# Attention's first loads all on SP's queue in the order of the jobs; ScalarE keeps only tables, rms_g and three weight chunks ahead of its copies

## Chip, cores, metric

One core of one Trainium2 chip. The metric is the device time of one execution in microseconds (us), median over runs. Engines: PE is TensorE's matmul, PEld its weight load, DVE VectorE, ACT ScalarE, POOL GpSimd, SP SyncE. ACT and SP both issue DMAs; "ACTq" and "SPq" are these issues in the profile. A load has landed when its data is in place and its completion counter says so; an engine stands when it waits at an instruction of its program.

## The reference, cut to what matters

```python
# attention: batch 8, heads 8, seq 576, head_dim 64, all float32
scores = scale * np.matmul(q, k.transpose(0, 1, 3, 2))
ret = scores * Dmat[None]            # decay gamma**(i-j) where i >= j, else 0
attn = np.matmul(ret, v)
# bridge to (4608, 512), then a gated FFN with d_ff 1536
xn = x / rms * rms_g
out = (silu(xn @ w_gate) * (xn @ w_val)) @ w_out
```

The weights reach the kernel as 64-bit floats (1 MB per chunk of 128 x 4 x 256), and DVE and ACT decode them to float32 on the chip.

## The kernel before: the parts that matter

Attention is cut into 32 jobs (one batch, two heads). The first four jobs load q and k untransposed, and PE transposes them; ACT copies the transposes out of PSUM. One core does the whole of it, with all instructions of an engine in program order.

```python
def load_first(j):                       # q, k of jobs 0..3: six DMAs, always on SP
    ...
    for nm, src in (("q", q), ("k", k)):
        for e in range(2):
            nc.sync.dma_start(out=st[j][nm][:, :, e], in_=src[b, 2*hp+e, :NFULL*P]...)
        nc.sync.dma_start(out=st[j][nm + "t"], in_=...)

def load_kv(j, queue):                   # here only v and its tail: four DMAs
    ...

def turn(j):                             # PE transposes, ACT copies, ACT scales v
    last = bank(...)
    for i, nm in enumerate("qk"):
        ps = bank(...)
        for c in range(NFULL):
            nc.tensor.transpose(out=ps[:, c*P:c*P+P], in_=d[nm][:, c]..., identity=ident)
        nc.tensor.transpose(out=last[:, o], in_=d[nm + "t"]..., identity=ident[:TAIL, :TAIL])
        nc.scalar.copy(out=t[:, :NFULL*P], in_=ps)
        nc.scalar.copy(out=t[:, NFULL*P:], in_=last[:, o])
    scale_v(j)

def load_chunk(i):                       # one 1 MB chunk of a weight, on ACT
    ...
    nc.scalar.dma_start(out=dst, in_=src[rws, cols].rearrange("(c p) f -> p c f", p=P))

def start():
    ...
    load_first(0)
    load_kv(0, nc.scalar)
    for i in (2, 3, 0, 1, 4):            # gv, gt, causal, causal_t, gc
        table(i)                         # on ACT
    load_first(1)
    load_chunks(1)                       # chunk 0
    load_kv(1, nc.scalar)
    load_first(2)
    table(5)                             # gq, 512 KB
    load_chunks(2)                       # chunk 1
    load_kv(2, nc.scalar)
    load_first(3)
    nc.scalar.dma_start(out=rms_g, in_=...)
    load_chunks(3)                       # chunk 2
    turn(0)                              # ACT's first copy stands here
    for j in range(NHP):
        slot(j)                          # scores, states, weighing, values of job j
        if j + 1 < NHP:
            turn(j + 1)
        ...                              # exponent(0), exponent(1) after slot 0: decoding starts
```

A DMA from ACT or SP has to take one of eight completion counters, which the compiled program gives out in turn to both queues. An issue stands until the load that held its counter before has landed. The packed trace holds the counter (semaphore) of every issue: eight of them, numbers 100 and 102 to 108, serve both queues in all kernels here.

## Time and profile before

| | before |
|---|---|
| median of 4 runs beside the changed kernel | 1278.45 us (1277.49 to 1279.64) |
| span of the profiled run | 1275.3 us |
| ACT's first copy | 28.05 us |
| first scores on PE | 29.30 us |
| first product of the up stage on PE | 76.68 us |
| start of PE's unbroken stretch | 164.32 us |

The last four rows are start times in the timelines, counted from the span's start. The last two are these lines of PE's timeline (start, length, engine and line, operation, count; in brackets the idle time before and what ended it):

```profile
76.68 12.29 PE L470 MATMUL up<-x,w_gate 128*128 128x384 f32 x32 [0.71 <-DVE x L382]
...
164.32 10.56 PE L470 MATMUL up<-x,w_gate 128*128 128x384 f32 x32 [0.80 <-ACT w_gate L548]
```

From the second of them on PE does not stop for anything worth naming until the end. These two marks serve as milestones: a gain at the start is a gain in the time only if it is still there at the second.

### The profile page before, as it was taken

Reading aid. Unit: us, or ns where it says so; the run is one execution under the profiler, and the core shown is the slowest. Engines: PE = TensorE matmul, PEld = TensorE weight load, DVE = VectorE, ACT = ScalarE, POOL = GpSimd, SP = SyncE. Lnnn points to the kernel's source line nnn. Section 1 sums busy time; section 2 is a strip of 40 time slices with the busy share of each in tenths; the row PEclk is TensorE's granted clock in tenths of the full one; section 3 lists DMA queues with packets and bytes.
Section 4 is the critical chain, followed back from the end, with each engine's and each line's share of the span. In section 5 each row is a group of like instructions: output and inputs, shape, how many; then the busy total and the mean of one; then the engine's idle time right before and its main releaser. Section 6 shows DMA issues by size and latency. Waiting matters only on the chain.

```text
span 1275.3 us, 16411 instructions
## 1 busy us (share of the span) xinstructions
PE 1219.4 (96%) x6792; PEld 925.8 (73%) x6792; DVE 547.5 (43%) x1056; ACT 280.0 (22%) x520; POOL 43.0 (3%) x44
## 2 busy tenths in 40 slices
PE   1789799999999999999999999999999999999998
PEld 1556555546985994985994995895895896795893
DVE  0679873013552553343453453343443443343340
ACT  1746452011120211211211221121121121111110
POOL 0000003140000000000000000000000000000000
PEclk9889799999999999999999999999999999999999
DMA  9448730022121132002112223002032100000000
GB/s 220 110 107 203 170 111 22 9 61 53 38 52 47 37 73 53 9 1 61 37 37 53 46 40 79 17 1 53 14 69 52 40 7 10 17 1 17 9 1 25
DMA packets 225307, 65.68 MB, mean 51 GB/s; under 512 B 212688, under 2 KB 212816, under 8 KB 225232
## 3 DMA queue, kind: packets, MB, share of 16 engines
q1 hardware_dynamic: 212224, 44.23, 17.1%
q10 hardware_dynamic: 13008, 20.39, 5.0%
q8 instruction: 53, 0.87, 0.3%
q14 instruction: 22, 0.18, 0.0%
HBM read 55.16 MB, written 9.44 MB: 51 GB/s over the span
## 4 chain that ended last, share of the span: by engine, by line
PE 88%; DVE 4%; DMA 3%; ACT 3%; issue 1%; ACTq 0%; POOL 0%; SPq 0%; DVEq 0%; POOLq 0%
PE out L484 29%; PE x L413 12%; PE w L413 12%; PE z L413 12%; PE up L470 6%; PE y L413 6%; PE s L242 3%; PE av L292 2%; PE av L306 2%; DMA w_out<-in_moe_w_gate_dram 1%; PE s L252 1%; DMA v<-in_v_dram 1%; PE ms L360 1%; ACT w_gate L548 1%; PE rb L380 1%
## 5 line engine op out<-in xcount | busy, mean ns | idle before, releaser
L484 PE MATMUL out<-w_out,h 128*128 128x512 f32 x792 | 346.1, 594 | 0.0
L484 PEld LDWEIGHTS out<-w_out,h 128*128 128x128 f32 x792 | 149.1, 190 | 177.5 <-issue 175.1
L489 ACT COPY o_all<-out 128x512 f32<-128x512 f32 x36 | 21.1, 585 | 348.9 <-PE out L484 334.9
L420 DVE TENSOR_TENSOR u<-m,y 128x384 f32<-128x384 f32 x60 | 33.2, 554 | 149.8 <-PE y L413 141.8
L264 DVE TENSOR_TENSOR ret<-s,causal 128x1024 f32<-128x1024 f32 x32 | 39.1, 1223 | 133.0 <-PE av L292 69.0
L413 PE MATMUL x<-x,w_gate 128*128 128x192 f32 x480 | 88.9, 328 | 1.5 <-ACT m L437 1.5
L413 PE MATMUL x<-x,w_val 128*128 128x192 f32 x480 | 89.1, 329 | 0.0
L413 PE MATMUL z<-x,w_gate 128*128 128x192 f32 x480 | 87.8, 326 | 0.0
L413 PE MATMUL w<-sums,w_val 128*128 128x192 f32 x480 | 87.8, 326 | 0.0
L413 PE MATMUL w<-sums,w_gate 128*128 128x192 f32 x480 | 87.8, 326 | 0.0
L413 PE MATMUL z<-x,w_val 128*128 128x192 f32 x480 | 87.8, 326 | 0.0
L413 PEld LDWEIGHTS x<-x,w_gate 128*128 128x128 f32 x480 | 79.2, 190 | 7.1 <-issue 4.3
L413 PEld LDWEIGHTS x<-x,w_val 128*128 128x128 f32 x480 | 78.8, 190 | 1.4 <-ACT m L437 1.4
L413 PEld LDWEIGHTS z<-x,w_gate 128*128 128x128 f32 x480 | 79.7, 190 | 0.0
L413 PEld LDWEIGHTS w<-sums,w_gate 128*128 128x128 f32 x480 | 79.7, 190 | 0.0
L413 PEld LDWEIGHTS w<-sums,w_val 128*128 128x128 f32 x480 | 79.7, 190 | 0.0
L413 PEld LDWEIGHTS z<-x,w_val 128*128 128x128 f32 x480 | 79.7, 190 | 0.0
L280 ACT ACTIVATE sd<-sum,gc 64x256 f32<-64x256 f32 x64 | 32.3, 504 | 200.2 <-DVE sum L274 199.8
L470 PE MATMUL up<-x,w_gate 128*128 128x384 f32 x192 | 67.8, 514 | 1.5 <-ACT w_gate L548 0.8
L420 DVE TENSOR_TENSOR h<-u,w 128x384 f32<-128x384 f32 x60 | 33.3, 554 | 81.4 <-PE w L413 81.4
L432 ACT ACTIVATE h<-h 128x384 f32<-128x384 f32 x90 | 47.0, 523 | 88.6 <-DVE h L420 88.6
L382 DVE SCALAR_TENSOR_TENSOR x<-x,rms_g,rb 128x384 f32<-128x384 f32 x48 | 26.3, 608 | 89.2 <-PE rb L380 89.2
(98 smaller groups left out, 1349.2 us busy)
## 6 DMA issues: line engine op xcount, KB each, us to landing
out_dram<-o_all SPq DMA_DIRECT2D x36, 256.0 KB, 2.0
k<-in_k_dram SPq DMA_DIRECT2D x64, 128.0 KB, 2.9
qraw<-in_q_dram SPq DMA_DIRECT2D x112, 72.0 KB, 2.4
kraw<-in_k_dram SPq DMA_DIRECT2D x112, 72.0 KB, 2.6
v<-in_v_dram SPq DMA_DIRECT2D x58, 128.0 KB, 2.8
w_out<-in_moe_w_gate_dram ACTq DMA_DIRECT2D x6, 1024.0 KB, 6.2
w_out<-in_moe_w_val_dram ACTq DMA_DIRECT2D x3, 1024.0 KB, 5.6
w_gate<-in_moe_w_val_dram ACTq DMA_DIRECT2D x3, 1024.0 KB, 5.7
```

Source lines behind the costliest of these rows:

```text
L242: nc.tensor.matmul(s[:, e, ck] if c < NFULL else s[e * n : e * n + n, 2, :n], lhsT=d["kT"][r, ck], rhs=d["qT"][r, ck], start=True, stop=True,)
L264: nc.vector.tensor_tensor(out=ret.rearrange("p e (c k) -> p e c k", c=NFULL), in0=s[:, :2].rearrange("p e (c k) -> p e c k", c=NFULL), in1 ...
L280: nc.scalar.activation(out=sd[j % 2][r, :, r], in_=t[r], func=AF.Copy, scale=gc[r, hp : hp + 1])
L292: nc.tensor.matmul(av[blk][e * D : e * D + D, o : o + n], lhsT=d["v"][:, c, e] if c < NFULL else d["vt"][r], rhs=d["ret"][:, e, c * P : c ...
L306: nc.tensor.matmul(av[blk][:, o : o + n], lhsT=sd[j % 2][:, c - 1], rhs=d["qT"][:, c * P : c * P + n], start=False, stop=(c in (AC - 1, NC ...
L382: nc.vector.scalar_tensor_tensor(out=x[:, c], in0=x[:, c], scalar=rms_g[:, c : c + 1], in1=rb[:, :U], op0=ALU.mult, op1=ALU.mult,)
L413: nc.tensor.matmul(ps[:, i * HU : i * HU + HU], lhsT=w_up[m][:, 2 * blk + c, cut], rhs=t_of[u][blk][:, c], start=(start and i == c == 0), ...
L420: nc.vector.tensor_tensor(out=o, in0=a, in1=pairs_of(ps), op=ALU.add)
L432: nc.scalar.activation(out=o, in_=c, func=AF.Silu)
L470: nc.tensor.matmul(ps[:, :U], lhsT=w_up[m][:, 4 * half + c, i * P : i * P + P], rhs=x_of[u][:, c], start=(c == 0), stop=(c == NHP - 1),)
L484: nc.tensor.matmul(ps[:, :DM], lhsT=h_of[u][:, f, s * P : s * P + P], rhs=w_out[:, f], start=(f == 0), stop=(f == NF - 1),)
L489: nc.scalar.copy(out=o, in_=ps[:, :DM])
```

## The change

Intent: SP issues all of attention's loads, in the order in which the jobs use them, and ACT gets to its first copy earlier.

```diff
-        load_first(0)
-        load_kv(0, nc.scalar)
+        for j in range(NHP):
+            load_first(j)
+            if j + 1 < NHP:
+                load_kv(j)              # now always on SP
         for i in (2, 3, 0, 1, 4):
             table(i)
-        load_first(1)
-        load_chunks(1)
-        load_kv(1, nc.scalar)
-        load_first(2)
+        load_chunks(2)
         table(5)
-        load_chunks(2)
-        load_kv(2, nc.scalar)
-        load_first(3)
         nc.scalar.dma_start(out=rms_g, in_=moe_rms_g.rearrange("(c p) -> p c", p=P))
         load_chunks(3)
         turn(0)
```

`load_kv` loses its `queue` argument and uses `nc.sync`.

## The prediction

> **What bounds the kernel now.** I read the page first (PE 96% busy), then a table of busy time over four stretches, which shows where the other 4% are. Its columns are the stretch in us, its length, then busy us (x instructions) of PE, PEld, DVE, ACT and POOL, the granted clock, the DMA share and GB/s.
>
> ```profile
> 0.00:29.00 29.00, 2.69 (x10) 1.78 (x10) 0.34 (x6) 2.23 (x4) 1.63 (x8) 1.00 0.95 217
> 29.00:77.00 48.00, 33.18 (x296) 26.66 (x296) 29.55 (x60) 30.47 (x54) 0.86 (x1) 0.85 0.36 90
> 77.00:165.00 88.00, 78.49 (x426) 50.18 (x426) 76.08 (x117) 47.38 (x64) 0.85 (x1) 0.89 0.77 185
> 165.00:1275.30 1110.30, 1105.07 (x6063) 847.13 (x6061) 441.50 (x875) 199.89 (x400) 39.67 (x34) 1.00 0.16 35
> ```
>
> From 165 us to the end PE is busy 1105 of 1110 us: that part is PE's and the change touches none of its instructions. The first 165 us are a start-up in which PE is idle for 29.00-2.69 = 26.3, then 14.8, then 9.5 us. In the first 29 us no compute engine does anything to speak of while the DMA engines are 95% busy. So the question is what keeps the compute engines waiting there. The chain of waits over the first 60 us, in order (start, length, what), says it:
>
> ```profile
> 0.73 0.51 ACTq L175
> ...
> 1.27 4.13 DMA v<-in_v_dram
> ...
> 7.54 5.97 DMA w_out<-in_moe_w_gate_dram
> ...
> 13.53 3.61 DMA h<-in_q_dram
> ...
> 17.16 6.76 DMA w_out<-in_moe_w_gate_dram
> ...
> 23.94 2.84 DMA v<-in_v_dram
> ...
> 26.78 1.26 ACT L203
> ...
> 28.05 0.58 ACT qT L203
> ```
>
> The timelines of ACT (its DMA issues and its first work) and of PE in the same stretch:
>
> ```profile
> 26.21 0.52 ACTq L528 DMA_DIRECT2D w_out<-in_moe_w_val_dram  x1
> 26.76 1.28 ACT L203 ACT_TABLE_LOAD   x1 [26.76 <-DMA v<-in_v_dram]
> 28.05 0.58 ACT L203 COPY qT<-turn_q 128x512 f32<-128x512 f32 x1
> ...
> 6.62 1.12 PE L193 MATMUL turn_k<-ident,k 128*128 128x128 f32 x4
> 28.81 0.36 PE L198 MATMUL turn_t<-ident,h 64*128 64x64 f32 x1 [21.07 <-ACT qT L204]
> ```
>
> PE has job 0's q and k transposed by 7.7 us, and then stands for 21.07 us because ACT has not copied them out of PSUM. ACT has not, because the copy stands in its program behind 22 DMA issues (v of three jobs, six tables, rms_g, three weight chunks), the last at 26.21. Each of those issues waits for one of eight completion counters that both queues use in turn, as the compiled order with its waits shows; so an issue on ACT stands until an older load, often a 1 MB chunk, has landed. The copy itself needs nothing that comes after 7.7 us.
>
> **What the Trainium skill says.**
> "DMA: Bandwidth & Descriptors", section "Anatomy of one DMA": a semaphore wait of a DMA is waited out on the issuing sequencer, not in the DMA engine. The trace agrees: ACT issues the second half of job 2's v at 23.94, 0.02 us after chunk 1, issued at 17.16, has landed (17.16 + 6.76), and nothing of ACT runs in the gap before it.
> Same page, "Issuing engines are not separate DMA queues": all issuers share the same 16 DMA engines, so moving a load between SP and ACT saves only sequencer time. Here it says that no bandwidth is gained: the DMA share is 0.95 in the first 29 us. What can be gained is the sequencer's blocking, and that is far more than issue time here.
> "ScalarE: Activation LUTs", "What ACT_TABLE_LOAD costs": about 1283 ns. The trace has 1.28 us between the last issue and the first copy; the change keeps it.
> "TensorE: Matmul & The Clock Gate", "The HAM clock gate": half clock after idle windows of about 3.4 us that run freely. The trace agrees in kind: four transposes take 1.08 to 1.12 us up to 35 us and 0.61 at 44 us. A start that is shifted meets these windows elsewhere.
>
> **The change, part by part.**
> Removed from ACT ahead of its first copy: 12 issues, four for each of jobs 0 to 2 (v in two halves, vt in two halves). By themselves they are 1.10 + 1.20, 1.10 + 1.82 and 2.37 + 1.18 us in ACT's timeline, some waits included, so under 9 us; what counts is that of the 18 issues that wait for a counter before the first copy, 5 are left.
> Added to SP: the same 12 issues, interleaved per job (q, k, v; then the next job). Total bytes, number of DMAs and everything after the start-up are the same: the comparison of the two compiled orders shows PE, DVE and POOL in the same order, SP 12 issues longer before v of job 3, ACT 12 shorter.
> Moved: chunk 1 now directly follows chunk 0; gq, rms_g, chunk 2 follow, then the copy.
>
> When does ACT reach its copy afterwards? The compiled order of the changed kernel gives its waits. Five tables: no wait. Chunk 0 waits for q of job 0, first half; chunk 1 for q's tail; gq for v of job 0, first half; rms_g for job 0's vt; chunk 2 for q of job 1, first half, and that load, on SP, waits in turn for chunk 0. So one chain of three landings sets it, with durations from the table of DMA issues:
> - q of job 0 issued at 0.74, landing 3.1 us later: 3.8. (The five tables need 0.34+0.34+0.48+0.69+0.45 plus gaps, 2.5 us from 0.73: 3.2, so they don't bind.)
> - chunk 0 issued at 3.8; its landing took 6.0 us before beside loads of the other queue (5.2 to 6.8 for the three chunks): 9.8.
> - q of job 1 issued at 9.8; such loads took 3.1 to 3.8 us alone and 5.0 to 6.4 beside a chunk; chunk 1 and gq (1.5 MB) are still on the way: 5.0, so 14.8.
> - chunk 2 issued at 14.8 instead of 26.21.
> The side waits come earlier: v of job 0 is issued near 5 and lands by 11, gq follows. Table load and copy keep their distance of 1.84 us, so the first copy is at about 16.6 instead of 28.05: **11.4 us earlier**.
>
> Does all that follow shift as well? From 28 to 77 us the chain is copies, scores, weighing, states, then DVE's decoding of the weights, all behind each other in program order. The inputs have to be there at the shifted times. Job 1's k, second half, waits for chunk 1 (issued near 5, behind chunk 0 in its queue, landing near 13.5) and lands near 18.5; PE wants it at 34.11-11.4 = 22.7. Job 1's v is issued near 15 to 16, lands near 21; ACT scales it at 37.85-11.4 = 26.4. Job 2's k waits for chunk 2 (near 20) and lands near 25; PE wants it at 44.7-11.4 = 33.3. Chunk 2 itself is first read at 53.28-11.4 = 41.9. Margins of 4 to 20 us: the shift is carried whole. Later loads are triggered by compute (SP's v of job 3 by PE's values of job 0, chunk 3 by ACT's place in its program), so they shift too. After 165 us PE runs without gaps, so what is gained stays gained. Sum: 1279.1 - 11.4 = 1267.7, and I say 1267.5.
>
> **Rivals.**
> 1. *The counters take the waits' place.* SP's loads now wait for ACT's chunks and ACT's last chunk for SP's loads. If each of the three landings is at its slow end (3.7, 6.8, 6.4), chunk 2 is issued at 17.6 and the gain is 8.6 us: 1270.5. If at the fast end (2.9, 5.2, 3.6), at 12.4 and 13.8: 1265. For the slow end: two chunks now stand back to back in one queue beside six loads of job 0. For the fast end: in before, ACT's own 0.26 MB of v travelled beside q at the beginning.
> 2. *Attention's data arrive late.* All 36 loads are now on one queue in order; if the DMA engines, not ACT, set the start-up, job 1 or 2 would stand at its transposes and most of the gain goes back: perhaps 5 us left, 1274. For it: DMA share 0.95, some 220 GB/s over 6.7 MB in 30 us. Against it: the bytes needed before the copy fall (v of jobs 1 and 2, q and k of jobs 2 and 3 move behind it), and the margins above.
> 3. *The gain is lost in the weights' stage.* From 77 to 165 us DVE is 86% busy, the DMA engines 77%, and PE waits for weights. If that stage started at a fixed time, because chunks come at the rate of the DMA engines, the earlier start would be absorbed: 1277. Against it: chunks 3 on are issued by ACT behind its own work, and the DMA share from 29 to 77 us is only 0.36, so the data wait for the program.
> 4. *The clock.* Before, PE ran at half speed to about 40 us, and again near 137 to 153 us. Windows that fall otherwise give or take about 2 us.
>
> **Range and chances.** Rival 1 spans 1265 to 1270.5; the clock and the spread of the runs before (1277.5 to 1279.6) widen it by about 2.5 each way: 1262.5 to 1273. Faster by over 2% needs 25.6 us, and the first copy cannot come before about 8 us, 20 us earlier than now: 2%. Slower by over 2% would need a new wait of 25 us in the long stretch, whose order is unchanged: 1%. Within 2%: 97%.
>
> **What the changed profile would show.** Right: the ACT table load at 13 to 17 us; chunk 2's issue just ahead of it, ended by q of job 1; PE's wait for the copy shrunk from 21.07 to about 10 us; the jobs' first scores, PE's first up product (76.68) and the start of the unbroken PE stretch all about 11 us earlier. Wrong: PE waiting for k or v of job 1 or 2 (rival 2); the first up product earlier but the unbroken stretch beginning at the same 165 us (rival 3); chunk 2 issued after 19 us (rival 1 beyond my span).

## The result

| | before | after |
|---|---|---|
| median of 4 runs | 1278.45 us | 1266.28 us (1264.60 to 1266.58) |
| ratio | | 0.9902, 95% interval 0.9884 to 0.9919 |
| span of the profiled run | 1275.3 | 1264.4 |
| ACT's first copy | 28.05 | 16.56 |
| first scores | 29.30 | 17.80 |
| first up product | 76.68 | 65.47 |
| start of the unbroken stretch | 164.32 | 153.39 |

A ratio here is the mean time of one kernel's fast runs over that of the other's of the same rounds, so it is not quite the ratio of the medians quoted. It is 1% faster clear of noise.

ACT's timeline after, up to its first copy:

```profile
3.27 2.15 ACTq L528 DMA_DIRECT2D w_out<-in_moe_w_gate_dram  x2
13.57 0.35 ACTq L617 DMA_DIRECT2D gq<-gq_table  x1
14.24 0.43 ACTq L631 DMA_DIRECT2D rms_g<-in_moe_rms_g_dram  x1
14.73 0.51 ACTq L528 DMA_DIRECT2D w_out<-in_moe_w_val_dram  x1
15.26 1.28 ACT L203 ACT_TABLE_LOAD   x1 [15.26 <-DMA h<-in_q_dram]
16.56 0.59 ACT L203 COPY qT<-turn_q 128x512 f32<-128x512 f32 x1
```

Ten issues instead of 22; the last, chunk 2, now at 14.73 instead of 26.21, and the timeline names what ended ACT's wait: a load of q. That is q of job 1, which SP issued when chunk 0 had landed. The trace's semaphores show this chain on counter 102: q of job 0 (landed at 3.20), chunk 0 (issued at 3.27, landed at 9.77), q of job 1 (issued at 9.79, landed at 14.71), chunk 2 (issued at 14.73). SP's timeline has q of job 1 at 9.79, and PE's timeline of the same kernel follows:

```profile
9.79 0.93 SPq L157 DMA_DIRECT2D h<-in_q_dram  x2
...
22.17 0.93 SPq L157 DMA_DIRECT2D h<-in_q_dram  x2
```

```profile
10.11 1.09 PE L193 MATMUL turn_k<-ident,k 128*128 128x128 f32 x4 [4.24 <-DMA k<-in_k_dram]
17.31 0.37 PE L198 MATMUL turn_t<-ident,h 64*128 64x64 f32 x1 [6.11 <-ACT qT L204]
...
22.29 0.63 PE L193 MATMUL turn_k<-ident,k 128*128 128x128 f32 x4
...
65.47 12.39 PE L470 MATMUL up<-x,w_gate 128*128 128x384 f32 x32 [0.71 <-DVE x L382]
...
153.39 10.56 PE L470 MATMUL up<-x,w_gate 128*128 128x384 f32 x32 [0.80 <-ACT w_gate L548]
```

PE waits 6.11 us for ACT instead of 21.07, but 4.24 us for k of job 0, which did not matter before. All milestones have moved by about the same: the first copy by 11.49, the first scores by 11.50, the first up product by 11.21, the unbroken stretch by 10.93. The table by stretch says the same of the engines (columns as in the prediction's first table, the borders moved by about 11 us):

```profile
0.00:17.60 17.60, 2.76 (x10) 1.79 (x10) 0.34 (x6) 2.33 (x4) 1.64 (x8) 1.00 0.88 231
17.60:66.00 48.40, 31.28 (x296) 25.21 (x296) 29.75 (x61) 30.44 (x54) 0.87 (x1) 0.79 0.54 135
66.00:154.00 88.00, 78.24 (x426) 50.09 (x425) 75.92 (x116) 47.34 (x64) 0.85 (x1) 0.89 0.78 185
154.00:1264.40 1110.40, 1105.14 (x6063) 847.15 (x6062) 441.61 (x875) 200.18 (x400) 39.69 (x34) 1.00 0.16 35
```

Only the first stretch has become shorter. The second has the same work; its DMA share rises from 0.36 to 0.54 as part of the first loads, which used to be over by then, now runs beside it.

### The profile page after: what moved, and what is told of

Read it like the earlier page. It is cut to its first block, busy times and chain, and to the rows that moved or that the text cites. A ratio compares the mean times of both kernels' runs of the same rounds, so it can differ in the third digit from the quotient of the medians.

```text
span 1264.4 us, 16414 instructions
## 1 busy us (share of the span) xinstructions
PE 1217.4 (96%) x6792; PEld 924.2 (73%) x6792; DVE 547.6 (43%) x1056; ACT 280.3 (22%) x520; POOL 43.0 (3%) x44
## 4 chain that ended last, share of the span: by engine, by line
PE 88%; DVE 5%; ACT 3%; DMA 2%; issue 1%; SPq 1%; POOL 0%; DVEq 0%; ACTq 0%; POOLq 0%
PE out L484 29%; PE x L413 12%; PE w L413 12%; PE z L413 12%; PE y L413 6%; PE up L470 6%; PE s L242 3%; PE av L292 2%; PE av L306 2%; PE s L252 1%; DMA k<-in_k_dram 1%; ACT w_gate L548 1%; PE ms L360 1%; DVE w_gate L572 1%; DMA v<-in_v_dram 1%
```

## The experiments

The theory under test: the time hangs on the moment at which ACT is through its issues and starts copying; ACT is held there by loads of the other queue through the shared counters; the shift is then carried whole to the end. The rivals: the order of the loads brings the gain, or the data being there earlier; part of the shift is lost in the weights' stage; the clock decides. The ten new kernels and the second run of the changed one (e11) gave correct results. e11 is the changed kernel in the rounds of e9 and e10; it was expected at 1265 to 1267.5 us with a first copy at 15.5 to 17.5, and both came true.

| kernel | first copy | first scores | first up product | unbroken from | span | median us | ratio to before (95%) |
|---|---|---|---|---|---|---|---|
| before | 28.05 | 29.30 | 76.68 | 164.32 | 1275.3 | 1278.45 | |
| after | 16.56 | 17.80 | 65.47 | 153.39 | 1264.4 | 1266.28 | 0.9902 (0.9884, 0.9919) |
| e11, after again | 16.30 | 17.54 | 64.72 | 152.31 | 1263.3 | 1265.05 | 0.9886 (0.9871, 0.9901) |
| e1, queue alone | 15.89 | 17.14 | 65.35 | 153.55 | 1264.6 | 1265.78 | 0.9895 (0.9880, 0.9909) |
| e2, order alone | 26.37 | 27.62 | 74.33 | 161.98 | 1273.3 | 1275.91 | 0.9976 (0.9960, 0.9993) |
| e6, ACT held longer | 31.67 | 32.89 | 80.82 | 169.10 | 1280.1 | 1281.61 | 1.0017 (1.0002, 1.0032) |
| e4, one chunk ahead | 5.64 | 12.51 | 62.72 | 151.04 | 1262.0 | 1263.75 | 0.9871 (0.9856, 0.9886) |
| e5, no chunk ahead | 5.18 | 7.80 | 67.54 | 155.48 | 1266.5 | 1268.31 | 0.9906 (0.9891, 0.9921) |
| e8, after with PE kept warm | 16.94 | 18.18 | 63.39 | 151.60 | 1262.6 | 1264.08 | 0.9873 (0.9856, 0.9889) |
| e9, all on SP | 5.67 | 7.65 | 60.70 | 148.56 | 1259.7 | 1261.76 | 0.9859 (0.9845, 0.9874) |
| e10, e9 with PE kept warm | 5.17 | 8.01 | 62.11 | 150.86 | 1261.9 | 1262.75 | 0.9863 (0.9847, 0.9880) |
| e12, all on SP, woven | 5.16 | 7.80 | 57.35 | 144.73 | 1255.7 | 1257.49 | 0.9831 (0.9818, 0.9845) |
| e13, chunks on GpSimd | 5.12 | 20.29 | 67.44 | 155.05 | 1265.9 | 1267.60 | 0.9907 (0.9894, 0.9921) |

Two columns subtracted say most of it. Span minus start of the unbroken stretch lies between 1110.85 and 1111.3 in all thirteen profiles; start of the unbroken stretch minus first up product between 87.4 and 88.8. So whatever a kernel gains up to the first up product it keeps to within 1.4 us. Only what lies before it has to be explained.

### e1: the queue alone

```diff
-        load_kv(0, nc.scalar)      # and the same for jobs 1 and 2;
+        load_kv(0, nc.sync)        # all else in the order of before
```

> The order of before, with v of jobs 0 to 2 issued on SP instead of ACT, and nothing else. Theory (what counts is when ACT is through its issues, set by the chain q of job 0, chunk 0, q of job 1, chunk 2): its compiled waits hold the same chain, only gq and chunk 1 have changed places, so the first copy comes at 15.5 to 17.5 us (changed kernel 16.56, before 28.05) and the time is 1265 to 1268. Rival (the order of the jobs' loads and of the tables brings the gain): the order is that of before, so 1274 to 1279.

First copy 15.89, time 1265.78, ratio 0.9895: the time of the changed kernel. Once v is off ACT's queue, the order of the jobs' loads and tables in the program brings nothing more; taking v off is what makes the gain.

### e2: the order alone

```diff
             if j + 1 < NHP:
-                load_kv(j)                 # the changed kernel's order,
+                load_kv(j, nc.scalar)      # v issued on ACT
```

> The order of the changed kernel, but v of jobs 0 to 2 back on ACT, at the head of its program. Theory: ACT has its 22 issues again, but the chunks come last, so the 12 of v do not wait for chunks; at eight loads under way and some 3.5 us each I put the last issue at 17 to 21 us, the first copy at 19 to 23, the time at 1269 to 1273: between the two kernels. Rival (only the queue counts): 1277 to 1280. Rival (only the order counts): 1265 to 1267.

A miss in size: first copy at 26.37, not 19 to 23, and time 1275.91, not 1269 to 1273. ACT's timeline shows why:

```profile
13.45 1.89 ACTq L528 DMA_DIRECT2D w_out<-in_moe_w_gate_dram  x2
...
24.53 0.52 ACTq L528 DMA_DIRECT2D w_out<-in_moe_w_val_dram  x1
25.08 1.28 ACT L203 ACT_TABLE_LOAD   x1 [25.08 <-DMA k<-in_k_dram]
```

I had counted only how fast eight loads at a time get through. Twelve issues of v in front of the five tables start chunk 0 at 13.45 instead of 3.27, 10.2 us later. From there to chunk 2's issue it takes 24.53 - 13.45 = 11.1 us here, and 14.73 - 3.27 = 11.5 us in the changed kernel, but not through the same chain: by the trace's semaphores chunk 2 waits here for q of job 3, which SP issued at 15.99 without waiting for a chunk, and which took 8.5 us to land beside chunks 0 and 1. So v at the head of ACT's queue costs the 10.2 us; that the rest takes as long is not one mechanism. The order alone does gain a little, 0.24% (0.07 to 0.40).

### e6: the changed kernel with ACT held longer

```diff
         load_chunks(3)
+        pad = temp("pad").rearrange("p (a b) -> p a b", b=P)
+        for _ in range(27):
+            nc.scalar.activation(out=pad, in_=ones.unsqueeze(1).to_broadcast([P, NS, P]),
+                                 func=AF.Copy, scale=1.0)
         turn(0)
```

> The changed kernel with 27 idle copies on ACT (some 0.42 us each, 11.4 us together) between its last DMA issue and the first copy; all loads as in the changed kernel. Theory (all that follows hangs on the first copy, the shift is carried whole): first copy at 28, time 1277 to 1279, as before. Rival (the gain is in the loads, attention's data or chunks being there earlier): some of the delay is caught up, 1266 to 1273.

ACT's timeline:

```profile
16.83 14.93 ACT L635 ACTIVATE pad<-ones 128x384 f32<-128x384 f32 x27
31.67 0.57 ACT L203 COPY qT<-turn_q 128x512 f32<-128x512 f32 x1
```

The pad took 14.93 us rather than the 11.4 that I had worked out, 0.55 us for each copy and not 0.42; that is why the time lies above the expected 1277 to 1279. So the first copy came at 31.67, 15.11 us later than in the changed kernel, and the span grew by 1280.1 - 1264.4 = 15.7 us. Nothing is caught up, although the loads ahead of the first copy are as early as in the changed kernel (chunk 2 is issued at 14.98 against 14.73). "The data being there earlier" is ruled out as the source of the gain; the start of ACT's copies is.

### e4 and e5: fewer chunks ahead of the copies

```diff
-        load_chunks(2)                    # e4: load_chunks(1); e5: nothing
-        table(5)
-        rms_g, load_chunks(3)
         turn(0)
+        load_chunks(2); table(5); rms_g; load_chunks(3)
```

> The changed kernel, with chunk 1, gq, rms_g and chunk 2 issued behind job 0's copies; only the five tables and chunk 0 ahead. Theory (time follows the first copies): ACT is free at 5 us, so k of job 0 (landed at 8.4 to 11.3 us in the runs so far) becomes the bound; first scores at 10 to 12.5 us instead of 17.80, time 1258 to 1262. Rival (the chunks are needed early, and what they are issued later comes back as DVE waiting for them): 1264 to 1268 in spite of early scores.

> The changed kernel with all three chunks, gq and rms_g behind job 0's copies and scaling. Theory: k of job 0 lands without a chunk beside it, near 6.5; first scores at 8 to 9.5 us, 8.5 us earlier than in the changed kernel; chunk 0 is issued near 10, lands near 16, at most 1 to 2 us after DVE wants it; time 1256.5 to 1260.5. Rival (chunks needed early): DVE waits for chunk 0 and 1 by more than 3 us, ACT stands at its issues before job 1's copies, time 1260 to 1266, no better than with one chunk ahead.

Both have their scores about as early as expected, 12.51 and 7.80. Both missed their times: e4 lies between its two ranges, and e5 is above both of its own: with its scores 10 us earlier it is no faster than the changed kernel. The line of job 0's `sd` (its scaled state, which ACT computes between job 0's copies and job 1's) in ACT's timeline, of e4 and of e5, after the issue of chunk 2:

```profile
21.16 0.50 ACTq L528 DMA_DIRECT2D w_out<-in_moe_w_val_dram  x1
21.76 1.02 ACT L280 ACTIVATE sd<-sum,gc 64x256 f32<-64x256 f32 x2 [8.15 <-DMA h<-in_q_dram]
```

```profile
25.31 0.37 ACTq L528 DMA_DIRECT2D w_out<-in_moe_w_val_dram  x1
25.79 1.02 ACT L280 ACTIVATE sd<-sum,gc 64x256 f32<-64x256 f32 x2 [16.89 <-DMA h<-in_k_dram]
```

ACT's stand has not gone; it has moved from ahead of job 0's copies to between job 0's and job 1's, 8.15 us in e4 and 16.89 in e5. The wait is ACT's, at an issue, for a counter: in e5 chunk 2's issue at 25.31 follows the landing of a load of job 2's k at 25.29 on the same counter. The rival, DVE waiting for late chunks, is not what happened in e4, where DVE waited 0.2 us for one. In e5 it did come true, and so did ACT's stand, which the same rival had named: DVE waited 1.98 and 6.13 us for chunks 0 and 1. DVE's timeline of e5:

```profile
22.63 0.69 DVE L544 TENSOR_SCALAR w_gate<-w_out 128x1024 uint32<-128x1024 uint32 x1 [6.13 <-DMA w_out<-in_moe_w_gate_dram]
```

That wait was over at 22.63 and ACT's only at 25.79, so ACT's is the one that held up job 1.

### e9 and e12: no chunk on ACT at all, in two orders on SP

```diff
-        nc.scalar.dma_start(out=dst, in_=...)                        # in load_chunk
+        (nc.sync if i < 3 else nc.scalar).dma_start(out=dst, in_=...)
-            nc.scalar.dma_start(out=t, in_=src.ap())                 # in table
+            (nc.sync if i == 5 else nc.scalar).dma_start(out=t, in_=src.ap())
# e9:  tables, job 0, job 1, chunks 0 1, q k of job 2, gq, v of job 2, job 3, chunk 2, rms_g
# e12: tables, job 0, chunk 0, job 1, chunk 1, q k of job 2, gq, v of job 2, chunk 2, job 3, rms_g
```

> The changed kernel, with chunks 0 to 2, gq and rms_g on SP too, in the order job 0, job 1, chunks 0 and 1, job 2's q and k, gq, job 2's v, job 3, chunk 2, rms_g; ACT issues only the five small tables before its copies and nothing between job 0's and job 1's. Theory (the time follows the first scores as long as ACT does not stand at an issue): first scores near 7.8 us as with no chunk ahead, ACT free of the 8 to 17 us stand ahead of sd of job 0, chunks 0 and 1 landing near 18 and 21, at most 1 to 2 us late for DVE; time 1256 to 1260. Rival (the chunks are needed early and their place on the queue, not ACT's stand, made the runs with late chunks lose): DVE waits for them, 1262 to 1268.

> As the run with all loads on SP, with the chunks woven in where they are wanted: job 0, chunk 0, job 1, chunk 1, job 2's q and k, gq, job 2's v, chunk 2, job 3, rms_g. In the former run DVE waited 4.62, 2.10 and 3.09 us for chunks 0, 1 and 2 and the first product of the up stage came at 60.70 instead of 65.47. If the order is what was wrong there, these waits shrink to under 4 us together and the time is 1257 to 1260.5; if the loads as a whole are the bound by then (6.7 MB in the first 37 us), the waits only change place: 1260.5 to 1263.

In e9 ACT does not stand at an issue any more, scores start at 7.65, and yet the time fell only to 1261.76, between the theory's range and the rival's (from 1262). The mechanism is the rival's: DVE waits for chunks. DVE's timeline of e9:

```profile
18.29 0.69 DVE L544 TENSOR_SCALAR w_gate<-w_out 128x1024 uint32<-128x1024 uint32 x1 [4.62 <-DMA w_out<-in_moe_w_gate_dram]
21.09 0.69 DVE L544 TENSOR_SCALAR w_gate<-w_out 128x1024 uint32<-128x1024 uint32 x1 [2.10 <-DMA w_out<-in_moe_w_gate_dram]
...
37.04 0.69 DVE L544 TENSOR_SCALAR w_gate<-w_out 128x1024 uint32<-128x1024 uint32 x1 [3.09 <-DMA w_out<-in_moe_w_val_dram]
```

So once ACT is out of the way, the loads themselves are the next bound, and their order counts. e12 weaves the chunks in where they are wanted. DVE's waits for DMAs, from its list of waits up to 66 us in e12:

```profile
DVE w_gate L544 <- DMA w_out<-in_moe_w_gate_dram: 5.7, 1, 5.7
...
DVE x L315 <- DMA gq<-gq_table: 1.2, 1, 1.2
```

The total is 6.9 us against 6.7 + 3.1 + 1.8 = 11.6 in e9 by the same list; chunks 1 and 2 are no longer waited for. First up product at 57.35, time 1257.49, ratio 0.9831: the best of all, 1.7% faster than before and clearly faster than the changed kernel (0.9886 to 0.9902). I had expected these waits under 4 us together; chunk 0 is still 5.7 us late, without the time being out of its range.

### e13: chunks on GpSimd's queue

```diff
-        nc.scalar.dma_start(out=dst, in_=...)                        # in load_chunk; gq and rms_g too
+        (nc.gpsimd if i < 3 else nc.scalar).dma_start(out=dst, in_=...)
```

> The changed kernel with chunks 0 to 2, gq and rms_g issued by GpSimd, whose loads share no counter with the other two queues, so that neither ACT nor SP waits for a chunk. Theory: ACT does not stand; 3.5 MB of chunks and gq run beside job 0's loads from about 3 us on, so k and v of job 0 land late, at 10 to 13 us; first scores at 11 to 14 us, no wait of DVE for chunks, time 1259 to 1263. If the counters did not matter and the landing of job 0's data alone did, the first scores come no earlier than in the changed kernel (17.80) and the time is 1265 to 1268.

A clear miss: scores and time are those of the expectation's second case, in which the landing of job 0's data sets them. No issue waits for a chunk (the trace has GpSimd's loads on counters of their own, 110 to 114), ACT is free at 3.3 us, and still the first scores come at 20.29. PE's timeline:

```profile
18.53 1.08 PE L193 MATMUL turn_k<-ident,k 128*128 128x128 f32 x4 [13.09 <-DMA k<-in_k_dram]
```

And the DMA view of e13 from 5 to 16 us, by queue (q0 is GpSimd's, q1 SP's; packets, MB, share of 16 engines):

```profile
q0 software_dynamic: 948, 3.51, 87.9%
q1 hardware_dynamic: 1338, 0.33, 13.7%
```

The two queues get packets in like numbers, but a GpSimd packet carries 3.51 MB / 948 = 3.7 KB and one of SP 0.25 KB, so SP gets a tenth of the bytes until GpSimd's are through. The counters, which hold ACT up, are also what kept all chunks from being in flight at once. Without that brake and without an order, the first job's k is last. SP was slowed as well: two of its issues took 4.2 us each although their counters were free; why, no run here shows. This does not make the data of job 0 the bound of the changed kernel: there k of job 0 was transposed from 10.11 on, and ACT's first copy came at 16.56.

### e8 and e10: PE kept at full clock

```diff
             ps = bank(f"turn_{j}_{nm}")
+            for _ in range((0, (48, 10, 8, 30)[j])[i]):    # e10: 0, 10, 8, 30
+                nc.tensor.transpose(out=ps[:, :P], in_=ident, identity=ident)
             for c in range(NFULL):
```

> The changed kernel with idle transposes on PE (48, 10, 8 and 30 of them ahead of k's transposes of jobs 0 to 3) that fill PE's waits; results unchanged. For the point of the clock: if the slow windows lie on the path, scores of jobs 0, 1 and 3 fall from 2.49 to 1.42 us and the time by 2 to 4 us (1262 to 1264.5); if the stretch is set by ACT and DVE whatever PE's clock, it is 1265.5 to 1267.

> The same with idle transposes on PE (10, 8 and 30, ahead of k's transposes of jobs 1 to 3). If the clock is worth what the run with them on the changed kernel says, 2 to 3 us less than without them: 1254 to 1257.5; if DVE and ACT are the bound now that they start earlier, the same within 1 us.

Job 1's scores, from PE's timelines of the changed kernel and of e8:

```profile
26.21 2.49 PE L242 MATMUL s<-qT,kT 64*128 64x128 f32 x20
```

```profile
26.59 1.42 PE L244 MATMUL s<-qT,kT 64*128 64x128 f32 x20 [0.22 <-ACT kT L205]
```

Job 1's and job 3's scores fell to 1.42; job 0's did not, and job 2's, which had been fast, became slow. From first scores to first up product e8 takes 63.39 - 18.18 = 45.21 us, the changed kernel 65.47 - 17.80 = 47.67: 2.5 us less, and 2.0 less than e11 (64.72 - 17.54 = 47.18). The time, 1264.08, is in the expected range, but the intervals of the ratios of e8, e11 and the changed kernel overlap, so a gain in the time is not shown. On e9 the same filling gains nothing (62.11 - 8.01 = 54.10 against 53.05), within the 1 us that was expected if PE's clock is off the path; DVE waits for chunks in both.

## Why the prediction was right, point by point

- **ACT's place in its program as the bound: right.** e6 moves nothing else and moves the time by as much; e1 shows that the queue of v alone does it; e4 and e5 show the same stand coming back at another place.
- **The chain of three landings: right as a sum, with two terms that offset each other.** Chunk 0 went at 3.27, not 3.8: q of job 0 landed at 3.20, after 2.46 us and not 3.1, just as ACT was through its tables (3.22). Chunk 0 took 6.52 us (3.27 to 9.79), not 6.0. q of job 1 took 4.94 (9.79 to 14.73), not 5.0. Chunk 2 at 14.73 against 14.8, first copy at 16.56 against 16.6. That the errors cancelled is luck.
- **The side waits: too early by 2.6 us, and not harmless.** I let v of job 0 land by 11 us; gq, which waits for it, was issued at 13.57. Behind it rms_g, which waits for job 0's vt (landed at 14.22), kept ACT until 14.24 + 0.43 = 14.67; q of job 1 landed at 14.71. In e11, e6 and e8, with the same loads, rms_g even ended last, by 0.02 to 0.07 us. So two chains end together here, not one; an earlier q of job 1 alone would have gained 0.04 us at most. That the second one did not come later is luck too.
- **Which loads ACT waits for: put too simply.** The prediction says that ACT often stands for a 1 MB chunk. Of the 18 waits in the kernel before, only one, v of job 2, was for a chunk directly; the others were for loads of q, k and v, some of which landed late beside a chunk (5.84 to 6.57 us beside chunk 0) or had waited for one.
- **k of job 0: not foreseen.** I took its landing from before (PE had transposed it by 7.7); with two chunks behind each other beside it, its second half landed at 9.98. It cost nothing as ACT came at 16.56 anyway, but in e4 it is what sets the scores. PE's wait that was to shrink to about 10 us came in two parts, 4.24 for k and 6.11 for ACT.
- **The margins: one was used up.** Job 1's k was to land at 18.5 with PE wanting it at 22.7. SP's next wait ended at 22.17, when its second half, issued at 14.37, had landed: 7.8 us, not 4 to 5. PE started those transposes at 22.29, just behind it. ACT was not free until 24.96, so the rival "attention's data arrive late" stayed off the path by 2 to 3 us, not by 4. Chunk 2 took 8.5 us and landed at 23.24, not near 20, far from its first use.
- **The shift carried whole: right.** First copy 11.49 earlier, unbroken stretch 10.93 earlier, so 0.56 us less. The weights' stage took 87.92 us between the two milestones against 87.64 before, so rival 3 is refuted. The 0.56 us is within what single profiles differ by: in e11, the same kernel, the first copy is 11.75 and the unbroken stretch 12.01 earlier.
- **Size.** Predicted 1267.5; the changed kernel ran at 1266.28 and, in another set of rounds, 1265.05. My working had the gain at 11.4 us; the profiled spans give 10.9, the ratio of the runs 0.0098 x 1278.45 = 12.5, with an interval of 10 to 15.
- **The bound for "over 2% faster": wrong in one figure.** The prediction says that the first copy cannot come before about 8 us; it came at 5.1 to 5.7 in e4, e5, e9, e10, e12 and e13. None of them was 2% faster.

## What to carry to other kernels

A DMA issue in the program of a compute engine is a wait like any other when completion counters are shared: look for the engine's first useful instruction, and for what the issues ahead of it wait on, including loads of another queue. Moving the issues to an engine without compute removes that wait; after that the order of the loads, by when each is wanted, is the next bound (e12 against e9), and issuing everything at once is not an order (e13). Check such a gain at a milestone far downstream before counting it.

## What the Trainium skill lacked or had wrong

- "DMA: Bandwidth & Descriptors", "Issuing engines are not separate DMA queues" says that several issuing engines save only the sequencer's issue time, "which is usually small relative to the DMA itself". For the DMA engines the runs agree: their busy share over the first 16 us is 0.89 in both kernels. What it lacks is an issuer with other work: ACT's issues and its waits at them set the start-up, with its first own instruction at 26.76 us before and 15.26 after, and stands of 8.15 and 16.89 us in e4 and e5, although one issue takes 0.3 to 0.7 us.
- No page that I read tells what it costs when loads of two queues take turns at a few completion counters, as this compiled program lets them: chunk 2 on ACT waited for q on SP, which waited for chunk 0 on ACT, 10.8 to 11.8 us from chunk 0's issue to chunk 2's in the five runs with this chain (changed kernel, e1, e6, e8, e11).
- "DMA: Bandwidth & Descriptors", "Queues, rings and completion order": engines go round between queues by packets. The runs agree in kind (changed kernel, 5 to 10 us: 727 packets of ACT's queue with 1.45 MB, 778 of SP's with 0.19 MB, from the DMA view, so 2 KB against 0.24 KB each), but the page does not draw the consequence for a load of 256-byte rows: 128 KB of k took 6.45 us beside two chunks and 15.1 us beside GpSimd's 3.5 MB, against 2.7 us in the median of e13's k loads.
- "ScalarE: Activation LUTs", "What ACT_TABLE_LOAD costs" gives 1283 ns plus a drain of 1380 ns. The 1.28 us agree; for this first load of the program no drain shows, the copy starts 0.02 us after the load ends (15.26 + 1.28 against 16.56).
- "TensorE: Matmul & The Clock Gate", "The HAM clock gate" has a half-rate state after idleness and a full-rate one: this case agrees in kind (the same scores in 2.49 and 1.42 us). Filling PE's waits with idle transposes shortened the stretch from first scores to first up product by 2.0 to 2.5 us in one profile (e8) and not at all where DVE waited for chunks (e10).
